# Channel DFT of an FNet plus Mixer layer: products by even and odd channel blocks of 162 columns, their sums on VectorE and GpSimd

## The chip, the cores and the metric

The kernel runs on one core of one Trainium2 chip. The metric is the device time of one execution in microseconds (us); where several runs are given, the median stands with the lowest and the highest beside it. The core has five engines, each with a queue of its own that it works off in order: TensorE (PE in the profile, with its weight loads as PEld), VectorE (DVE), ScalarE (ACT), GpSimd (POOL) and SyncE (SP, which only issues DMA transfers here). Engines wait for each other by semaphores.

## The reference, cut to what matters

The input x has S = 2048 rows (tokens) and D = 640 channels, F is 1728, and everything is fp32:

```python
xn = layernorm(x)
a = einsum("bsd,ed->bse", xn, dft_hid_re)         # DFT along the channels
b = einsum("bsd,ed->bse", xn, dft_hid_im)
fnet = einsum("ts,bse->bte", dft_seq_re, a) - einsum("ts,bse->bte", dft_seq_im, b)
h = layernorm(xn)
u = gelu(einsum("bsd,sf->bdf", h, w1) + b1)       # the MLP runs along the tokens
out = x + fnet + (einsum("bdf,fs->bds", u, w2) + b2).transpose(0, 2, 1)
```

So the output is x, plus the real part of a two-dimensional DFT of the normalized rows, plus a two-layer MLP that mixes tokens.

## The kernel before

**Precision.** An fp32 product is made of three products of a 1-pass type (fp32r). Each matrix is cut into a high part, which ScalarE rounds (`high`, L130), and a low part, the difference, which VectorE makes (`low`, L133). `three` (L138 to L140) then issues high by high, high by low, low by high into one PSUM bank. Every row "PE L138", "L139" or "L140" is one such matmul, and "PEld" of the same line is its weight load.

**Stages.** TensorE runs through them in order: the up projection (w1, with the LayerNorm ahead of it) to about 203.5 us of the profile; the sequence DFT, to 222.7; the channel DFT, to 245.4; the down projection (w2) with the sum of all three terms, to 437.7; then the last rows are stored. The kernel takes the matrices of the reference as inputs and uses the symmetries of DFT matrices: only parts of them are used in the products, and all through the run other parts are loaded and compared with what symmetry says of them (tiles `check`, lines 895 to 983). If one of these comparisons failed, a general version would run at the end.

**The program's order.** Work is a list of `steps`. Step i issues, in this order: its entries of `loads` (DMA), of `reads`, the ScalarE cut for step i + 2, the entries of `middle`, the VectorE cut for step i + 2, the entries of `measures` and `behind`, and last the matmuls of step i. Since every engine works in order, this list fixes what stands behind what in each queue. Entries are put there by `at(step, function, when=list)`.

**The channel DFT** (`hid_step`, `hid_products`). The sequence DFT leaves folded sums in five blocks T0 to T4 (tiles `t_cut`), the moving operand is the channel matrix. Rows and channels have mirror symmetries, so a quarter of the rows suffices: four blocks of 128 rows, named by (odd, i), in the order (1, 0), (1, 1), (0, 0), (0, 1). Each block takes two steps, s = 0 and s = 1, and each step fills two banks (part 0, cosine, and part 1, sine). A bank has 324 columns, 162 for even and 162 for odd channels, and 9 products: `three` by T2 (mixed), by T0 or T3, and by T1 or T4. To make whole rows of 324 columns, each of the four matrices q in `hid_main` is held twice, the second time with alternating sign; the second copy is made by ScalarE on L646 while the sequence DFT runs. In the third block one more bank of 9 products, two rows high, makes the first and the middle row of the output (`mid_bank`, `y_mid`).

**Behind a block.** `copies` (ScalarE, L705) brings both banks of s = 1 to SBUF (tile `sums`), `sums` (VectorE, L709 to L712) makes sum and difference of s = 0 and s = 1, `whole_rows` (VectorE, L663 to L666) turns each into a row block of 640 channels (tile `y`). `read` stores it by SyncE for s = 0 and scatters it by an indirect DMA of GpSimd for s = 1 (L670); `read_back` has ScalarE write it backwards (L727), which is the mirrored row block, and scatters (s = 0) or stores it (s = 1). `read_mid` (ScalarE, L740) does the same for the two special rows. All of it stands two to four steps behind the block's first step, so for the later blocks in the down projection's first steps.

**The down projection.** Sixteen output blocks t of four steps each; a block has 82 products of 320 columns, numbered below by f = 0 to 13, the 128-row slices of w2 (six products for each f, four for f = 13, the short last slice whose low half is stacked beneath). A step needs its cut piece of w2 (`piece`, L130 and L133, from `w_raw`) and the cut of the gelu output, `h_cut0` to `h_cut6`, two slices f each: `h_high` (ScalarE) and `h_low` (VectorE). `h_cut4`, `h_cut5` and `h_cut6` are cut at the end of the channel DFT and in the first two steps of the down projection; GpSimd zeroes 64 rows of `h_cut6` for f = 13 behind its VectorE cut (`h_tail`, L775). Each output block reads its `y` rows back from DRAM (`rest`), adds x, adds the projection (L828, L833) and is stored.

The lines that fix these places:

```python
at(step + 2, copies, when=reads)
at(step + 2, sums, when=reads)
at(step + 2, read(0), when=reads)
at(step + 3, read(1), when=reads)
at(step + 3, read_back(0))
at(step + 4, read_back(1))
order = [(odd, i) for odd in (1, 0) for i in range(NJ)]
at(s_down + 2, h_tail)
```

Of the kernel before, what the change touches and what calls it, by code (L numbers as in the profile page):

```python
# [16 lines left out]
P = 128  # L17
# [32 lines left out]
def fnet_plus_mixer(  # L50
# [579 lines left out]
    def hid_high(q):  # L630
        if not hid_cut:
            hid_cut.append(keep.tile([P, 2, 4, 2, EW], R32, name="hid_main", tag="zt"))
# [3 lines left out]
        nc.scalar.activation(hid_main[:, 0, q, 0], raw[:, q], AF.Copy, scale=by)  # L636
        nc.scalar.activation(hid_mix[:, 0, q], raw[:, 4], AF.Identity, scale=mask[:, q : q + 1])

    def hid_low(q):
        hid_main, hid_mix = hid_cut  # L640
        raw, by = hid_place[0], -1.0 if q > 1 else 1.0
        for to, hi, of, times in (
            (hid_main[:, 1, q, 0], hid_main[:, 0, q, 0], q, by), (hid_mix[:, 1, q], hid_mix[:, 0, q], 4, mask[:, q : q + 1])
        ):
            nc.vector.scalar_tensor_tensor(to, raw[:, of], times, hi.bitcast(F32), op0=ALU.mult, op1=ALU.subtract)
        nc.scalar.activation(hid_main[:, :, q, 1], hid_main[:, :, q, 0].bitcast(F32), AF.Copy, scale=-1.0 if q % 2 else 1.0)  # L646
# [4 lines left out]
    def y_place(n):  # L651

        if n not in y_tiles:
            if n % 6 < 2:
                t = keep.tile([P, 2, 2 * D + 1], F32, name=f"y{n}", tag="n3")
                y_tiles[n - n % 2], y_tiles[n - n % 2 + 1] = t[:, 0], t[:, 1]
# [4 lines left out]
    def whole_rows(y, a, b, e=EW):  # L661
        v = nc.vector
        v.tensor_add(y[:, : e4 + 1], a[:, : e4 + 1], b[:, : e4 + 1])  # L663
        v.tensor_sub(y[:, e4 + 1 : 2 * e4], a[:, e + e4 - 1 : e : -1], b[:, e + e4 - 1 : e : -1])
        v.tensor_add(y[:, 2 * e4 : 3 * e4 + 1], a[:, e : e + e4 + 1], b[:, e : e + e4 + 1])
        v.tensor_sub(y[:, D : 3 * e4 : -1], a[:, :e4], b[:, :e4])  # L666
# [7 lines left out]
    def hid_products(to, w, part, all_blocks=True):  # L674
# [10 lines left out]
    def hid_step(n, odd, i):  # L685
# [16 lines left out]
        def copies():  # L702
            held.append(keep.tile([P, 4, 2 * EW], F32, name=f"sums{n}", tag=f"n{1 + n % 2}"))
# [9 lines left out]

        def read(s):
            def run():
                t, (y, back) = held[0], y_place(2 * n + s)
# [36 lines left out]
        if n == N_MID:  # L753
            at(step + 2, read_mid, when=reads)
# [595 lines left out]
```

## Time and profile before

| what | us |
|---|---|
| median of 3 runs (lowest, highest) | 445.84 (445.72, 446.01) |
| the profiled execution | 445.79 |
| its span, first to last instruction | 443.9 |
| TensorE's granted clock in it, mean | 0.998 |
| sequence DFT, 203.5 to 222.7: TensorE busy of 19.2 | 18.75 |
| channel DFT, 222.7 to 245.4: busy of 22.7: TensorE, VectorE, ScalarE, GpSimd | 22.70, 17.27, 12.44, 4.51 |
| down projection, 245.4 to 437.7: busy of 192.3: the same four | 192.30, 142.74, 96.01, 31.73 |

All times of the profile are of one execution, counted from its first instruction; 1.89 us of the execution lie outside the span. A row by time gives start, length, engine, line, operation, tile written and tiles read; an idle time in brackets at its end is that of the engine just before it, with the engine that ended it. In a row of a group, the number behind x counts instructions, then come busy time and mean ns of one, then idle time. Matmul lengths are modelled and overlap: the distance from one start to the next tells what a matmul takes. The clock row of the page (40 slices) shows 9 throughout, so durations of all stages can be set beside each other.

### The profile page before, as it was taken

The numbers are of one execution on the slowest core, as the hardware profiler recorded it, in microseconds if no ns is written. First come the engines' busy times: TensorE is split into PE (matmuls) and PEld (weight loads), VectorE is DVE, ScalarE is ACT, GpSimd is POOL, SyncE is SP. The second block draws the span as 40 slices with busy tenths as digits, with TensorE's granted clock in tenths as the row PEclk, the third lists the DMA queues.
The fourth block names the chain that finished last, engine by engine and source line by source line (L and its number), as shares of the span: only waits on it lengthen the run. The fifth ranks groups of instructions, "written<-read, shape, count | busy, mean of one in ns | idle before, by whom it ended". The sixth has DMA issues, their size and how long they took to land.

```text
span 443.9 us, 8043 instructions
## 1 busy us (share of the span) xinstructions
PE 434.4 (98%) x2955; PEld 426.8 (96%) x2955; DVE 321.0 (72%) x662; ACT 244.5 (55%) x467; POOL 78.8 (18%) x113
## 2 busy tenths in 40 slices
PE   8999999999999999999999999999999999999994
PEld 4899999999999999999999999999999999999993
DVE  5986634659677787778877947777777769688771
ACT  5566664565656655469645634646455454556440
POOL 2055525710000001100002420102202304101000
PEclk9999999999999999999999999999999999999999
DMA  8692506998665571312107999999998999979401
GB/s 294 222 358 77 189 2 182 312 403 318 199 224 193 190 227 49 117 51 87 46 31 272 291 382 402 397 398 370 329 377 308 313 374 325 376 268 354 149 31 38
DMA packets 49728, 105.71 MB, mean 238 GB/s; under 512 B 7285, under 2 KB 8197, under 8 KB 49681
## 3 DMA queue, kind: packets, MB, share of 16 engines
q1 hardware_dynamic: 46112, 93.53, 60.1%
q0 software_dynamic: 3424, 11.43, 7.1%
q8 instruction: 25, 0.41, 0.4%
q14 instruction: 23, 0.18, 0.1%
q10 hardware_dynamic: 144, 0.16, 0.1%
HBM read 94.60 MB, written 10.51 MB: 237 GB/s over the span
## 4 chain that ended last, share of the span: by engine, by line
PE 79%; DVE 6%; ACT 5%; DMA 3%; issue 3%; POOL 2%; SPq 0%; ACTq 0%; POOLq 0%; DVEq 0%
PE psum L138 25%; PE psum L139 25%; PE psum L140 25%; PE psum L813 2%; DMA w_raw<-in_w 2%; ACT zt L225 2%; DMA xp<-in_x 2%; DVE st L197 1%; POOL r L210 1%; DVE x L133 1%; DVE t L133 1%; ACT q L205 1%; ACT piece L130 1%; PE psum L273 1%; DVE early L133 1%
## 5 line engine op out<-in xcount | busy, mean ns | idle before, releaser
L133 DVE TENSOR_TENSOR piece<-w_raw,piece 128x512 fp32r<-128x512 f32 (+2 forms) x128 | 76.5, 598 | 79.6 <-ACT piece L130 78.2
L138 PE MATMUL psum<-h_cut,piece 128*128 128x320 f32 x416 | 128.6, 309 | 0.0
L140 PE MATMUL psum<-h_cut,piece 128*128 128x320 f32 x416 | 128.4, 309 | 0.0
L139 PE MATMUL psum<-h_cut,piece 128*128 128x320 f32 x416 | 128.3, 308 | 0.0
L130 ACT ACTIVATE piece<-w_raw 128x512 fp32r<-128x512 f32 (+1 forms) x112 | 66.5, 599 | 99.1 <-PE psum L140 57.9
L138 PE MATMUL psum<-x,piece 128*128 128x320 f32 x288 | 88.9, 309 | 0.0
L140 PE MATMUL psum<-x,piece 128*128 128x320 f32 x288 | 88.9, 309 | 0.0
L139 PE MATMUL psum<-x,piece 128*128 128x320 f32 x288 | 88.8, 308 | 0.0
L932 ACT ACTIVATE check<-check 128x1024 f32<-128x1024 f32 (+2 forms) x66 | 65.1, 987 | 34.1 <-DVE check L913 13.4
L138 PEld LDWEIGHTS psum<-h_cut,piece 128*128 128x128 f32 x416 | 78.1, 188 | 0.0
L140 PEld LDWEIGHTS psum<-h_cut,piece 128*128 128x128 f32 x416 | 78.1, 188 | 0.0
L139 PEld LDWEIGHTS psum<-h_cut,piece 128*128 128x128 f32 x416 | 78.1, 188 | 0.0
L273 PE MATMUL psum<-x,early 128*128 128x320 f32 x384 | 58.8, 311 | 2.0 <-DVE early L133 1.1
L273 PEld LDWEIGHTS psum<-x,early 128*128 128x128 f32 x384 | 56.3, 188 | 4.3 <-DVE early L133 1.6
L140 PEld LDWEIGHTS psum<-x,piece 128*128 128x128 f32 x288 | 54.1, 188 | 0.0
L138 PEld LDWEIGHTS psum<-x,piece 128*128 128x128 f32 x288 | 54.1, 188 | 0.0
L139 PEld LDWEIGHTS psum<-x,piece 128*128 128x128 f32 x288 | 54.1, 188 | 0.0
L895 POOL DMA_INDIRECT check<-in_dft_seq,from_seq x16 | 19.7, 1229 | 117.3 <-ACT check L932 114.9
L133 DVE TENSOR_TENSOR x<-zt,x 128x640 fp32r<-128x640 f32 x16 | 13.2, 823 | 12.2 <-ACT x L130 11.5
L670 POOL DMA_INDIRECT y<-y,to_mirror x8 | 9.2, 1146 | 62.0 <-DVE y L666 55.3
L833 DVE SCALAR_TENSOR_TENSOR rest<-psum,b_sb,rest 128x320 f32<-128x320 f32 x32 | 16.1, 544 | 1.0 <-PE psum L813 1.0
L828 DVE TENSOR_TENSOR rest<-rest 128x640 f32<-128x640 f32 x16 | 13.2, 822 | 3.3 <-DMA rest<-in_x 3.1
(197 smaller groups left out, 616.8 us busy)
## 6 DMA issues: line engine op xcount, KB each, us to landing
check<-in_dft_seq SPq DMA_DIRECT2D x58, 512.0 KB
w_raw<-in_w SPq DMA_DIRECT2D x56, 256.0 KB
w_raw<-in_w SPq DMA_DIRECT2D x32, 448.0 KB
rest<-y SPq DMA_DIRECT2D x16, 320.0 KB
rest<-in_x SPq DMA_DIRECT2D x16, 320.0 KB
out<-rest SPq DMA_DIRECT2D x15, 320.0 KB
ck<-in_dft_seq SPq DMA_DIRECT2D x6, 512.0 KB
xp<-in_x SPq DMA_DIRECT2D x8, 320.0 KB
```

Source lines behind the costliest of these rows:

```text
L130: nc.scalar.activation(hi, src, AF.Copy)
L133: nc.vector.tensor_sub(lo, src, hi.bitcast(F32))
L138: nc.tensor.matmul(bank, wh, mh, start=first, stop=False, skip_group_check=True)
L139: nc.tensor.matmul(bank, wh, ml, start=False, stop=False, skip_group_check=True)
L140: nc.tensor.matmul(bank, wl, mh, start=False, stop=last, skip_group_check=True)
L225: nc.scalar.activation(hi if direct else exact[k], rows[k], AF.Identity, scale=by, bias=add)
L273: nc.tensor.matmul(up_banks[f][half][:, :H2], w_cut[f, k // G][part == 2][:, c], n[:, part == 1, k % 2, half * H2 : (half + 1) * H2], star ...
L670: nc.gpsimd.indirect_dma_start(to, bass.IndirectOffsetOnAxis(ap=to_mirror[:, j : j + 1], axis=0), y, None,)
L828: nc.vector.tensor_add(rest[t][:, 0], rest[t][:, 0], rest[t][:, 1])
L833: nc.vector.scalar_tensor_tensor(rest[t][:, 1, cols], down_banks[t][half][:, :H2], b2_sb[:, t : t + 1], rest[t][:, 0, cols], op0=ALU.add, ...
L895: nc.gpsimd.indirect_dma_start(to[:, c * CH : (c + 1) * CH], None, dft_seq.rearrange("c k p t -> (c k p) t"), bass.IndirectOffsetOnAxis(ap ...
L932: nc.scalar.activation(v, v, AF.Square, accum_out=off[:, n : n + 1])
```

## The change

Products are made for each half of a bank apart. `hid_main` holds each matrix once (L646 is gone). T0 (or T3) goes to columns 0 to 161 alone, the even channels, T1 (or T4) to columns 162 to 323, the odd ones: six products of 162 columns. T2 follows with three of 324 columns, with masks that hold the even rows for one half and the odd rows for the other; two more one-column products make these masks at the start.

Now a bank holds an even and an odd part, and sum and difference of the two give the rows. `by_channels` makes them behind `sums`: one addition and one subtraction of 324 columns for part 0 on VectorE and for part 1 on GpSimd (L717, L718). `whole_rows` shrinks from four operations of 159 to 161 columns to two of 320 and 322 (L663, L665). For the two special rows there is one ScalarE copy (L742), two GpSimd sums (L747, L748) and two reversing copies (L751). The tile `sums` has six slots in place of four and other places in SBUF, and `h_cut4` to `h_cut6` too.

The blocks come in another order, (1, 0), (0, 0), (1, 1), (0, 1), so the special rows come with the second block. `read` and `read_back` stand one step later than before for the first two blocks, two for the third and three for the fourth, and each at the end of its step. Two kinds of comparison at the start of the down projection load two and four steps later.

```diff
-        nc.scalar.activation(hid_main[:, :, q, 1], hid_main[:, :, q, 0].bitcast(F32), AF.Copy, scale=-1.0 if q % 2 else 1.0)
...
-    def whole_rows(y, a, b, e=EW):
-        v = nc.vector
-        v.tensor_add(y[:, : e4 + 1], a[:, : e4 + 1], b[:, : e4 + 1])
-        v.tensor_sub(y[:, e4 + 1 : 2 * e4], a[:, e + e4 - 1 : e : -1], b[:, e + e4 - 1 : e : -1])
-        v.tensor_add(y[:, 2 * e4 : 3 * e4 + 1], a[:, e : e + e4 + 1], b[:, e : e + e4 + 1])
-        v.tensor_sub(y[:, D : 3 * e4 : -1], a[:, :e4], b[:, :e4])
+    def whole_rows(y, a, b):
+        back = y[:, D:e4:-1].rearrange("p (h e) -> p h e", h=3)[:, ::2]
+        nc.vector.tensor_sub(back, a[:, :, :e4], b[:, :, :e4])
+        to = y[:, :D].rearrange("p (h e) -> p h e", h=2)
+        nc.vector.tensor_add(to[:, :, : e4 + 1], a[:, :, : e4 + 1], b[:, :, : e4 + 1])
...
-        mix, both = hid_mix[:, :, 2 * part : 2 * part + 2], hid_main[:, :, 2 * part : 2 * part + 2]
-        for block, m in (
-            (T2, mix.rearrange("p h q e -> p h (q e)")), ((T0, T3)[part], both[:, :, 0].rearrange("p h s e -> p h (s e)")),
-            ((T1, T4)[part], both[:, :, 1].rearrange("p h s e -> p h (s e)")),
-        ):
-            three(to, w(block), [m[:, j] for j in range(2)], block == T2, block == (T1, T4)[part])
+        for h, block in enumerate(((T0, T1), (T3, T4))[part]):
+            three(to[:, h * EW : (h + 1) * EW], w(block), [hid_main[:, j, 2 * part + h] for j in range(2)], h == 0, False)
+        m = hid_mix[:, :, 2 * part : 2 * part + 2].rearrange("p h q e -> p h (q e)")
+        three(to, w(T2), [m[:, j] for j in range(2)], False, True)
...
-            held.append(keep.tile([P, 4, 2 * EW], F32, name=f"sums{n}", tag=f"n{1 + n % 2}"))
+            held.append(keep.tile([P, 6, 2 * EW], F32, name=f"sums{n}", tag=("n1", "n2", "n0", "zt")[n]))
...
+        def by_channels():
+            a = held[0].rearrange("p s (h e) -> p (s h) e", h=2)
+            for part, v in enumerate((nc.vector, nc.gpsimd)):
+                even, o = (a[:, 4 * part + h : 4 * part + 4 : 2] for h in range(2))
+                v.tensor_add(a[:, 8 + 2 * part : 10 + 2 * part], even, o)
+                v.tensor_sub(o, even, o)
...
+        def mid_copy():
+            mid = keep.tile([P, D + 2 * EW], F32, name="y_mid", tag="ck1")[0:2]
+            nc.scalar.activation(mid[:, D:], mid_bank[0], AF.Copy)
...
+            nc.gpsimd.tensor_add(y[:, : e4 + 1], even, o)
+            nc.gpsimd.tensor_sub(y[:, 2 * e4 : 3 * e4 + 1], even, o)
...
-        at(step + 2, read(0), when=reads)
-        at(step + 3, read(1), when=reads)
-        at(step + 3, read_back(0))
-        at(step + 4, read_back(1))
+        last = step + (0, 3, 3, 4, 5)[n + 1]
+        at(last - 1, by_channels)
+        for s in range(2):
+            at(last + s, read(s), when=behind)
+            at(last + s + 1, read_back(s))
         if n == N_MID:
-            at(step + 2, read_mid, when=reads)
-
-    order = [(odd, i) for odd in (1, 0) for i in range(NJ)]
+            at(step + 2, mid_copy, when=reads)
+            at(step + 3, read_mid)
+
+    order = [(odd, i) for i in range(NJ) for odd in (1, 0)]
...
-        n = keep.tile([P, 2, 2, D], R32, name=f"h_cut{i}", tag=f"n{(4, 5, 6, 7, 0, 1, 2)[i]}")
+        n = keep.tile([P, 2, 2, D], R32, name=f"h_cut{i}", tag=f"n{(4, 5, 6, 7, 1, 2, 3)[i]}")
...
-            nc.vector.tensor_mul(mask[:, i + 1 : i + 2], mask[:, i : i + 1], parity[:, 2:3])
+            nc.vector.tensor_mul(mask[:, i + 1 : i + 2], mask[:, i : i + 1], parity[:, 1:2])
+            nc.vector.tensor_mul(mask[:, i : i + 1], mask[:, i : i + 1], parity[:, 0:1])
...
-    at(begin, lambda: held_rows.append(quarter_check()), when=loads)
-    at(begin + 3, lambda: quarter_measure(held_rows[0]), when=behind)
+    at(begin + 4, lambda: held_rows.append(quarter_check()), when=loads)
+    at(begin + 6, lambda: quarter_measure(held_rows[0]), when=behind)
...
-        i = begin + 4 + 8 * n
+        i = begin + 6 + 8 * n
```

Three places in the engines' queues follow, each as line, operation, tile written, tiles read and shape. The tiles `sums0` to `sums3` and the `y` tiles are counted by block, two y tiles to a block.

ScalarE at the end of the channel DFT, before: from the copies of the second block to the first piece of w2 cut in the last step but one.

```order
L705 ACTIVATE sums1_2675<-psum3_101 128x324
L705 ACTIVATE sums1_2675<-psum4_102 128x324
L727 ACTIVATE y0_2626<-y0_2626 128x640
L727 ACTIVATE y2_2682<-y2_2682 128x640
L705 ACTIVATE sums2_2745<-psum0_98 128x324
L705 ACTIVATE sums2_2745<-psum1_99 128x324
L740 ACTIVATE y_mid_2758<-psum5_103 2x161
L740 ACTIVATE y_mid_2758<-psum5_103 2x159
L740 ACTIVATE y_mid_2758<-psum5_103 2x161
L740 ACTIVATE y_mid_2758<-psum5_103 2x159
L130 ACTIVATE piece_2765<-w_raw_134 128x512
```

The same place now:

```order
L703 ACTIVATE sums1_2677<-psum4_102 128x324
L703 ACTIVATE sums1_2677<-psum5_103 128x324
L742 ACTIVATE y_mid_2684<-psum1_99 2x324
L733 ACTIVATE y0_2655<-y0_2655 128x640 x2
L751 ACTIVATE y_mid_2684<-y_mid_2684 2x159 x2
L703 ACTIVATE sums2_2745<-psum0_98 128x324
L703 ACTIVATE sums2_2745<-psum1_99 128x324
L130 ACTIVATE piece_2752<-w_raw_134 128x512
```

The third block's copies (`sums2`) stand behind both reversed row blocks of the first block and behind the two `y_mid` copies, which read what GpSimd writes.

GpSimd from the third block's scatters to its MEMSET for `h_cut6`, before:

```order
L670 DMA y1_92<-y5_2788,to_mirror_81 514x640
L670 DMA y3_94<-y4_2752,to_mirror_81 514x640
L670 DMA y1_92<-y6_2830,to_mirror_81 514x640
L670 DMA y3_94<-y6_2830,to_mirror_81 514x640
L775 MEMSET h_cut6_2882 64x640
```

And now, from the first block's second scatter to the MEMSET:

```order
L669 DMA y1_92<-y0_2655,to_mirror_81 514x640
L747 TENSOR_TENSOR y_mid_2684<-y_mid_2684 2x161
L748 TENSOR_TENSOR y_mid_2684<-y_mid_2684 2x161
L669 DMA y3_94<-y2_2721,to_mirror_81 514x640
L669 DMA y1_92<-y3_2757,to_mirror_81 514x640
L717 TENSOR_TENSOR sums2_2745<-sums2_2745 128x324
L718 TENSOR_TENSOR sums2_2745<-sums2_2745 128x2x162
L669 DMA y3_94<-y4_2824,to_mirror_81 514x640
L669 DMA y1_92<-y5_2863,to_mirror_81 514x640
L717 TENSOR_TENSOR sums3_2812<-sums3_2812 128x324
L718 TENSOR_TENSOR sums3_2812<-sums3_2812 128x2x162
L788 MEMSET h_cut6_2859 64x640
```

The MEMSET stood behind the last scatter of all; now the fourth block's two sums stand ahead of it, and that block's two scatters behind it.

VectorE from the cut for the down projection's third step to the low half of `h_cut6`, before:

```order
L133 TENSOR_TENSOR piece_2836<-w_raw_134,piece_2836 128x512
L133 TENSOR_TENSOR h_cut5_2840<-h5_1932,h_cut5_2840 128x1280
L663 TENSOR_TENSOR y6_2830<-sums3_2823 128x161
L664 TENSOR_TENSOR y6_2830<-sums3_2823 128x159
L665 TENSOR_TENSOR y6_2830<-sums3_2823 128x161
L666 TENSOR_TENSOR y6_2830<-sums3_2823 128x160
L133 TENSOR_TENSOR piece_2878<-w_raw_134,piece_2878 128x256
L133 TENSOR_TENSOR piece_2878<-w_raw_134,piece_2878 64x128
L133 TENSOR_TENSOR h_cut6_2882<-h6_2353,h_cut6_2882 128x1280
```

And now, with the two sums behind it:

```order
L133 TENSOR_TENSOR piece_2819<-w_raw_134,piece_2819 128x512
L663 TENSOR_TENSOR y4_2824<-sums2_2745 128x2x160
L665 TENSOR_TENSOR y4_2824<-sums2_2745 128x2x161
L133 TENSOR_TENSOR h_cut5_2821<-h5_1934,h_cut5_2821 128x1280
L133 TENSOR_TENSOR piece_2855<-w_raw_134,piece_2855 128x256
L133 TENSOR_TENSOR piece_2855<-w_raw_134,piece_2855 64x128
L663 TENSOR_TENSOR y5_2863<-sums2_2745 128x2x160
L665 TENSOR_TENSOR y5_2863<-sums2_2745 128x2x161
L133 TENSOR_TENSOR h_cut6_2859<-h6_2351,h_cut6_2859 128x1280
L717 TENSOR_TENSOR sums3_2812<-sums3_2812 128x324
L718 TENSOR_TENSOR sums3_2812<-sums3_2812 128x2x162
```

Between these two cuts stand the rows of the third block in place of those of the fourth, four operations in place of four, but each twice as wide.

More of the change, by code (lines that the diff above doesn't have):

```diff
@@ L631, in hid_high @@
         if not hid_cut:
-            hid_cut.append(keep.tile([P, 2, 4, 2, EW], R32, name="hid_main", tag="zt"))
+            hid_cut.append(keep.tile([P, 2, 4, EW], R32, name="hid_main", tag="zt"))
             hid_cut.append(keep.tile([P, 2, 4, EW], R32, name="hid_mix", tag="ck0"))
@@ L635, in hid_high @@
         raw, by = hid_place[0], -1.0 if q > 1 else 1.0
-        nc.scalar.activation(hid_main[:, 0, q, 0], raw[:, q], AF.Copy, scale=by)
+        nc.scalar.activation(hid_main[:, 0, q], raw[:, q], AF.Copy, scale=by)
         nc.scalar.activation(hid_mix[:, 0, q], raw[:, 4], AF.Identity, scale=mask[:, q : q + 1])
@@ L642, in hid_low @@
         for to, hi, of, times in (
-            (hid_main[:, 1, q, 0], hid_main[:, 0, q, 0], q, by), (hid_mix[:, 1, q], hid_mix[:, 0, q], 4, mask[:, q : q + 1])
+            (hid_main[:, 1, q], hid_main[:, 0, q], q, by), (hid_mix[:, 1, q], hid_mix[:, 0, q], 4, mask[:, q : q + 1])
         ):
             nc.vector.scalar_tensor_tensor(to, raw[:, of], times, hi.bitcast(F32), op0=ALU.mult, op1=ALU.subtract)
-        nc.scalar.activation(hid_main[:, :, q, 1], hid_main[:, :, q, 0].bitcast(F32), AF.Copy, scale=-1.0 if q % 2 else 1.0)
     e4 = D // 4
@@ L653, in y_place @@
         if n not in y_tiles:
-            if n % 6 < 2:
+            if n < 2:
                 t = keep.tile([P, 2, 2 * D + 1], F32, name=f"y{n}", tag="n3")
-                y_tiles[n - n % 2], y_tiles[n - n % 2 + 1] = t[:, 0], t[:, 1]
+                y_tiles[0], y_tiles[1] = t[:, 0], t[:, 1]
             else:
@@ L712, in sums @@
             v.tensor_sub(t[:, 3], t[:, 3], banks[1])
+        def by_channels():
[4 more added lines that the diff above has]
+                v.tensor_sub(o, even, o)
         def read(s):
             def run():
-                t, (y, back) = held[0], y_place(2 * n + s)
-                whole_rows(y, t[:, s], t[:, 2 + s])
+                a, (y, back) = held[0].rearrange("p s (h e) -> p (s h) e", h=2), y_place(2 * n + s)
+                whole_rows(y, a[:, 8 + s : 2 * s : s - 7], a[:, 10 + s : 4 + 2 * s : s - 5])
                 if s:
@@ L732, in read_back @@
             return run
+        def mid_copy():
+            mid = keep.tile([P, D + 2 * EW], F32, name="y_mid", tag="ck1")[0:2]
+            nc.scalar.activation(mid[:, D:], mid_bank[0], AF.Copy)
+            mid_bank.append(mid)
         def read_mid():
-            a, y = mid_bank[0], keep.tile([P, D], F32, name="y_mid", tag="ck1")[0:2]
-            for to, of in (
-                (y[:, : e4 + 1], a[:, : e4 + 1]), (y[:, 2 * e4 - 1 : e4 : -1], a[:, EW + 1 : EW + e4]),
-                (y[:, 2 * e4 : 3 * e4 + 1], a[:, EW : EW + e4 + 1]), (y[:, D - 1 : 3 * e4 : -1], a[:, 1:e4]),
-            ):
-                nc.scalar.activation(to, of, AF.Copy)
+            y, (even, o) = mid_bank[1][:, :D], (mid_bank[1][:, D + h * EW :][:, : e4 + 1] for h in range(2))
+            nc.gpsimd.tensor_add(y[:, : e4 + 1], even, o)
+            nc.gpsimd.tensor_sub(y[:, 2 * e4 : 3 * e4 + 1], even, o)
+            for h in range(2):
+                begin = 2 * e4 * h
+                nc.scalar.activation(y[:, D - 1 - begin : 3 * e4 - begin : -1], y[:, begin + 1 : begin + e4], AF.Copy)
             for s in range(2):
```

2 lines of the change are left out of this document (1 added, 1 removed).

## The prediction

> **What bounds the kernel now.** Read first the page's busy times, then the chain of work that ended last, in order of time, then TensorE's rows by time.
>
> ```profile
> PE 434.4 (98%) x2955; PEld 426.8 (96%) x2955; DVE 321.0 (72%) x662; ACT 244.5 (55%) x467; POOL 78.8 (18%) x113
> ```
> ```profile
> 222.54 0.36 PE psum L592 x3
> 256.94 0.58 PE psum L813 x4
> ```
>
> The chain (start, length, engine, line) runs from 222.54 to 256.94 us without another engine's row: the whole channel DFT and the first output block are TensorE's alone. So what TensorE saves there ends the kernel sooner, as long as nobody else becomes late. TensorE's own rows (start, length, line, operation, in brackets the idle time before) give the spacing:
>
> ```profile
> 206.28 0.39 PE L139 MATMUL psum<-piece,f 128*128 128x256 f32 x1 [0.36 <-DVE piece L133]
> ...
> 213.24 0.28 PE L138 MATMUL psum<-piece,f 128*128 128x256 f32 x1
> ...
> 217.46 0.28 PE L138 MATMUL psum<-piece,f 128*128 128x258 f32 x1
> ...
> 222.74 0.31 PE L138 MATMUL psum<-hid_mix,t 128*128 128x324 f32 x1
> ...
> 245.36 0.31 PE L138 MATMUL psum<-h_cut,piece 128*128 128x320 f32 x1
> ...
> 255.90 0.31 PE L138 MATMUL psum<-h_cut,piece 128*128 128x320 f32 x1
> ```
>
> A row's length overlaps its neighbours; spacing is what counts. The channel DFT holds 17 banks of 9 products, 153 in (245.36 - 222.74) us: 0.1478 us for one of 324 columns. The 36 of 256 columns from 213.24 to 217.46 take 0.1172 us each. The last row is f = 12 of the first output block, 72 products of 320 columns behind 245.36: 0.1464 us each.
>
> **TensorE's part.** Six of a bank's nine products fall from 324 to 162 columns: 96 short ones in 16 banks and 6 in the bank for the middle row. No matmul under 256 columns of this type is in the trace. By columns alone a short one would be spaced 0.1478 x 162/324 = 0.074 us. But each has its own weight load:
>
> ```profile
> L140 PEld LDWEIGHTS psum<-hid_main,t 128*128 128x128 f32 x32 | 6.0, 188 | 0.0
> ...
> L139 PEld LDWEIGHTS psum<-hid_main,t_mid_cut 128*2 128x2 f32 x2 | 0.2, 84 | 0.1
> L592 PEld LDWEIGHTS psum<-own 65*65 65x65 f32 x1 | 0.1, 135 | 0.0
> ```
>
> From 2 to 128 columns a load (mean ns behind the bar) grows by (188 - 84)/126 = 0.83 ns a column, so 128 columns may hold the load path 0.106 us whatever streams past; loads do keep up at 0.117 us, as the 256-column rows show. I take 0.112 us, between these two, and 0.08 us in the middle bank, whose loads are two columns wide. A bank then costs 6 x 0.112 + 3 x 0.148 = 1.115 us in place of 1.33, and TensorE's part is 96 x 0.036 + 6 x 0.068 = 3.9 us shorter. Bounds: 0.074 us (7.5 us saved) and, if loads and products stop overlapping, the 0.188 us of a load (4.1 us lost).
>
> The four negating copies on ScalarE go too. One row each of ScalarE and VectorE by time:
>
> ```profile
> 201.36 0.47 ACT L646 ACTIVATE hid_main<-hid_main 128x324 fp32r<-128x324 f32 x1 [0.69 <-DVE hid_main L645]
> ```
> ```profile
> 204.13 1.49 DVE L133 TENSOR_TENSOR h_cut<-h,h_cut 128x1280 fp32r<-128x1280 f32 x1 [0.48 <-ACT h_cut L130]
> ```
>
> The copy kept ScalarE 0.69 us waiting and some 0.4 us busy; behind it ScalarE cuts the h_cut for which VectorE idles 0.48 us, and behind that comes the piece for which TensorE idles 0.36 us at 206.28. I count that 0.36 us as gone, bound below by nothing: the channel DFT starts at 222.38. Two more one-column mask products lie near 69 us, where TensorE has work queued: nothing.
>
> So TensorE alone would be 4.2 us ahead at 241.15. **What is late next** decides how much of it stays.
>
> **The engines behind.** POOL did no sums before. Its nearest rows (mean ns), and its stretch by time:
>
> ```profile
> L212 POOL TENSOR_SCALAR again<-mv,again 128x1 f32<-128x1 f32 x11 | 2.9, 262 | 1.1
> ...
> L775 POOL MEMSET h_cut<- 64x640 f32 x1 | 0.6, 633 | 0.0
> ...
> L407 POOL MEMSET zt<- 128x4 f32 x2 | 0.1, 102 | 0.0
> ```
> ```profile
> 244.89 0.97 POOL L670 DMA_INDIRECT y<-y,to_mirror  x1 [5.41 <-DVE piece L133]
> 246.16 1.10 POOL L670 DMA_INDIRECT y<-y,to_mirror  x1 [0.30 <-ACT sums L705]
> 252.44 0.97 POOL L670 DMA_INDIRECT y<-y,to_mirror  x1 [5.18 <-DVE y L666]
> 253.72 2.13 POOL L670 DMA_INDIRECT y<-y,to_mirror  x1 [0.30 <-ACT h_cut L130]
> 255.89 0.63 POOL L775 MEMSET h_cut<- 64x640 f32 x1
> ```
>
> A MEMSET grows by (633 - 102)/636 = 0.83 ns a column, 0.27 us for 324; on top of the 0.26 us of an arithmetic instruction a sum takes 0.53 us with one such pass, 1.07 with three (two reads, one write). I take two passes, 0.8 us. The Trainium skill's GPSIMD Engine Reference (3.1 Elementwise) states about 2.6 cycles at 1.2 GHz an element for a two-input add; an estimate from that is 0.70 us for 324 and a gain 0.3 us larger than below; no run here shows it yet. A scatter holds POOL 1.3 us (252.44 to 253.72).
>
> VectorE's rows by time for the stretch that matters:
>
> ```profile
> 242.61 0.69 DVE L133 TENSOR_TENSOR piece<-w_raw,piece 128x512 fp32r<-128x512 f32 x1
> 243.21 0.33 DVE L663 TENSOR_TENSOR y<-sums 128x161 f32<-128x161 f32 x1
> ...
> 246.34 0.48 DVE L709 TENSOR_TENSOR sums<-psum,sums 128x324 f32<-128x324 f32 x1
> ...
> 248.19 0.32 DVE L663 TENSOR_TENSOR y<-sums 128x161 f32<-128x161 f32 x1
> ...
> 253.51 1.49 DVE L133 TENSOR_TENSOR h_cut<-h,h_cut 128x1280 fp32r<-128x1280 f32 x1 [0.69 <-ACT h_cut L130]
> 254.92 0.69 DVE L133 TENSOR_TENSOR piece<-w_raw,piece 128x512 fp32r<-128x512 f32 x1
> ```
>
> From start to next start: a piece 0.60 us, the four sums of two banks 1.85, an h_cut 1.41. The new 320 to 324 column operations lie between 0.38 (by columns of the piece) and 0.46 (a quarter of the four sums): 0.41. Note the slack before: h_cut6 is ready at 254.9, TensorE wants it at 255.90. One microsecond. If TensorE comes four earlier, VectorE is late.
>
> Now the queues as the change orders them. The third block's ScalarE copies stand behind both reversed rows of the first block and two y_mid copies that wait for POOL. TensorE ends the second block (with the middle bank) at 222.38 + 8 x 1.115 + 0.92 = 232.2. ScalarE copies it and the middle bank, and reverses the first row by 233.8. POOL: scatter to 235.15, two sums to 236.75, scatter to 238.05, two short y_mid sums (0.8 together) to 238.85. ScalarE's y_mid copies (0.2 each) and its first copy of the third block end at 239.7. So VectorE starts the third block's sums at 239.75, though TensorE had the block ready at 236.7. They end at 241.6, the first piece at 242.2: TensorE starts the down stage at 242.3, not at 241.15.
>
> Then VectorE's queue without rest: two row sums 0.82, two channel sums 0.82, piece 0.60, about 0.5 idle until ScalarE has cut h_cut4, h_cut4 1.41, four sums 1.88, piece 0.61, rows 0.82, h_cut5 1.41, split piece 0.63, rows 0.82: from 242.25 to 252.6; h_cut6 to 254.0. TensorE can start f = 12 at 254.05 and f = 13 six products later, if the rows of POOL's MEMSET are there. POOL: scatter behind the rows of 252.6, to 253.9; the fourth block's two sums, to 255.5; MEMSET 0.63, to 256.2. TensorE starts f = 13 at 256.25. Before it did so at 255.90 + 6 x 0.1464 = 256.78. **Of 4.2 us there remain 0.5.** Behind that the stage is TensorE's again, with the same products as before.
>
> The same count with other values: POOL's sum at 0.53 us gains 1.6, at 1.07 it loses 0.6. Short products at 0.074 us gain 2.0, and 3.2 with POOL at 0.53; at 0.117 nothing. Transfers: the same bytes; the second block of w2 moves behind one y store, to about 238, and is wanted at 247; the first check loads move two to four steps later. Nothing.
>
> The sum is made on the profiled execution, 445.79 us with a span of 443.9; the median is 445.84. 445.79 - 0.5 = **445.3 us**.
>
> **Rivals.**
> 1. *VectorE and POOL hold each other up*, 446.7 us. Speaks for it: the scatter beside the h_cut of 253.51 lasted 2.13 us, not 0.97. Against: others beside VectorE's work, 244.89 among them, were not longer. Place: the third block's two POOL sums fall beside the piece and h_cut4. If VectorE stands for them, 1.6 us less its 0.5 idle, h_cut6 ends at 255.0; the fourth block's two sums take turns with h_cut6 and one channel sum: 255.0 + 0.8 + 0.41 + 0.8 + 0.63 = 257.6, f = 13 is 0.9 later than before. Decides from the point where the held time passes 0.5 us. With sums of 0.53 it gains 0.8 (445.0), with 1.07 it loses 2.9 (448.7). The Trainium skill's SBUF — State Buffer (Who interferes with whom) states just this: a VectorE instruction with two SBUF inputs and a GpSimd instruction that reads SBUF exclude each other for a whole instruction. By that page the time would be the 446.7 of this rival; no run here has shown such a pair.
> 2. *Short products are not shorter*, 447.3 to 461.5 us. Nothing of this width is in the trace, so a spacing of its own can't be excluded. At 0.148 us TensorE saves nothing and the queue behind it still costs 1.5. At 0.311, the whole length of a 324-column row, 96 x 0.163 = 15.7 us are lost. Decides from 0.148 us. Against it: spacing follows columns from 320 to 256.
> 3. *The queue behind is shorter than counted*, 442.6 to 444 us: POOL near 0.5 us, short products near 0.074, no turns taken. Then 1.8 to 3.2 us stay.
>
> **Chances.** The forecast (444.6 to 446.4, POOL's bounds) 0.45, rival 1 0.28, rival 2 0.15, rival 3 0.12. The range takes in all but rival 2's greater part and the outer ends: 442.6 to 448.7. A difference of 0.2%, 0.9 us, is about what a measurement tells from none. Faster by more: two fifths of the forecast, all of rival 3, a little of rival 1: 0.32. Slower by more: half of rival 1, rival 2, a little of the forecast: 0.30. Within: 0.38.
>
> **What would show it.** Right: spacing of the 162-column rows near 0.11 us; the channel stage about 19 us long; idle time of TensorE before the first piece, before h_cut5 or h_cut6 and before f = 13 of the first output block, released by VectorE and POOL; none later. Wrong: short rows at 0.15 us or more; POOL sums far from 0.8 us; VectorE's rows longer than before beside POOL's sums (rival 1); no idle time at all (rival 3); idle time in later output blocks, for which I see no cause.

## The result: slower by 0.94%, and the profile after

The changed kernel takes 450.16 us (median of 6 runs, 448.33 to 451.33), the kernel before 445.86 us (6 runs, 445.72 to 446.12): ratio 1.0094, 95% interval 1.0072 to 1.0116. That is above the whole range of the prediction, and on the other side of no change than its forecast. The profiled execution took 451.33 us with a span of 449.5 us and a mean clock of 0.989.

First the page's busy times, then the view by stretches. Its columns are the stretch, its length, the busy time and count of TensorE, its weight loads, VectorE, ScalarE and GpSimd, then the granted clock, the DMA share and GB/s.

```profile
PE 435.1 (97%) x2955; PEld 426.3 (95%) x2955; DVE 328.9 (73%) x656; ACT 243.8 (54%) x462; POOL 88.6 (20%) x123
222.30:241.20 18.90, 18.90 (x155) 18.45 (x153) 15.24 (x35) 8.62 (x24) 6.43 (x8) 1.00 0.18 71
241.20:259.50 18.30, 12.88 (x80) 11.60 (x79) 17.96 (x27) 9.18 (x14) 9.29 (x9) 0.98 0.84 282
259.50:265.90 6.40, 6.38 (x24) 6.38 (x25) 4.47 (x9) 1.37 (x2) 2.30 (x2) 0.51 1.02 393
```

The channel DFT fills TensorE and is shorter (18.9 us; 22.7 before). In the first output block the roles are turned: VectorE is busy 17.96 of 18.30 us, TensorE 12.88. And in the next 6.4 us, with TensorE busy again, its clock is 0.51.

TensorE's rows by time (start, length, line, operation, idle time before; "..." stands for rows left out):

```profile
222.41 0.28 PE L139 MATMUL psum<-hid_main,t 128*128 128x162 f32 x1
222.52 0.28 PE L140 MATMUL psum<-hid_main,t 128*128 128x162 f32 x1
...
241.37 0.38 PE L138 MATMUL psum<-h_cut,piece 128*128 128x320 f32 x1 [0.16 <-DVE sums L708]
242.80 0.41 PE L140 MATMUL psum<-h_cut,piece 128*128 128x320 f32 x1 [0.91 <-DVE piece L133]
...
250.76 0.42 PE L140 MATMUL psum<-h_cut,piece 128*128 128x320 f32 x1 [0.66 <-DVE piece L133]
...
253.10 0.41 PE L139 MATMUL psum<-h_cut,piece 128*128 128x320 f32 x1 [0.46 <-DVE h_cut L133]
...
256.21 0.41 PE L139 MATMUL psum<-h_cut,piece 128*128 128x320 f32 x1 [1.10 <-DVE h_cut L133]
...
257.05 0.31 PE L826 MATMUL psum<-h_cut,piece 128*128 128x320 f32 x1
259.52 1.17 PE L826 MATMUL psum<-h_cut,piece 128*128 128x320 f32 x3 [2.17 <-POOL h_cut L788]
260.49 0.47 PE L138 MATMUL psum<-h_cut,piece 128*128 128x320 f32 x1
260.75 0.47 PE L139 MATMUL psum<-h_cut,piece 128*128 128x320 f32 x1
...
265.93 0.31 PE L138 MATMUL psum<-h_cut,piece 128*128 128x320 f32 x1
```

Short products start 0.11 us apart. The down projection starts at 241.37, 3.99 us earlier than before (245.36). Then come five more stalls in its first block, each released by VectorE or, the longest, by GpSimd's MEMSET of `h_cut6` (L788). The first product of f = 13 needs only the high half and runs at 257.05; the second needs the zeroed rows and runs at 259.52, where all four had started at 256.78 before. From 260.49 on products start 0.27 us apart in place of 0.15; at 265.93 the usual length is back.

VectorE's and GpSimd's rows of that stretch:

```profile
234.69 1.64 DVE L663 TENSOR_TENSOR y<-sums 128x320 f32<-128x320 f32 x1
...
244.53 1.74 DVE L133 TENSOR_TENSOR piece<-w_raw,piece 128x512 fp32r<-128x512 f32 x1
246.20 2.04 DVE L133 TENSOR_TENSOR h_cut<-h,h_cut 128x1280 fp32r<-128x1280 f32 x1
...
254.26 0.50 DVE L665 TENSOR_TENSOR y<-sums 128x322 f32<-128x322 f32 x1
254.67 1.49 DVE L133 TENSOR_TENSOR h_cut<-h,h_cut 128x1280 fp32r<-128x1280 f32 x1
256.07 0.49 DVE L717 TENSOR_TENSOR sums<-sums 128x324 f32<-128x324 f32 x1
256.60 1.56 DVE L718 TENSOR_TENSOR sums<-sums 128x324 f32<-128x324 f32 x1
258.08 1.24 DVE L133 TENSOR_TENSOR piece<-w_raw,piece 128x512 fp32r<-128x512 f32 x1
```
```profile
237.58 0.99 POOL L669 DMA_INDIRECT y<-y,to_mirror  x1 [0.64 <-DVE y L665]
...
244.96 0.77 POOL L717 TENSOR_TENSOR sums<-sums 128x324 f32<-128x324 f32 x1
245.80 1.10 POOL L718 TENSOR_TENSOR sums<-sums 128x324 f32<-128x324 f32 x1
...
255.03 1.97 POOL L669 DMA_INDIRECT y<-y,to_mirror  x1 [1.14 <-DVE y L665]
257.03 0.76 POOL L717 TENSOR_TENSOR sums<-sums 128x324 f32<-128x324 f32 x1
257.87 0.90 POOL L718 TENSOR_TENSOR sums<-sums 128x324 f32<-128x324 f32 x1
258.83 0.63 POOL L788 MEMSET h_cut<- 64x640 f32 x1
```

Beside GpSimd's sums of 244.96 and 245.80 (the third block's) a piece lasts 1.74 us in place of 0.69 and the cut of `h_cut4` 2.04 in place of 1.49. VectorE's own sum beside the one of 257.03 lasts 1.56 us, its neighbour 0.49, and the piece of 258.08 lasts 1.24 (0.69 is usual). The row operation of 234.69 stands beside the second block's sums on GpSimd (235.20 and 236.05) and lasts 1.64 us, where 0.49 is usual; the scatter of 237.58 waits 0.64 us for these rows. At the end the MEMSET follows a scatter of 1.97 us and two sums.

### The profile page after: what moved, and what is told of

It reads as the page before. It is cut to its first block, busy times and chain, and to the rows that moved or that the text cites. A ratio compares the mean times of both kernels' runs of the same rounds, so it can differ in the third digit from the quotient of the medians.

```text
span 449.5 us, 8052 instructions
## 1 busy us (share of the span) xinstructions
PE 435.1 (97%) x2955; PEld 426.3 (95%) x2955; DVE 328.9 (73%) x656; ACT 243.8 (54%) x462; POOL 88.6 (20%) x123
## 4 chain that ended last, share of the span: by engine, by line
PE 82%; DVE 6%; DMA 4%; issue 2%; ACT 2%; POOL 1%; POOLq 0%; ACTq 0%; DVEq 0%
PE psum L138 23%; PE psum L139 23%; PE psum L140 23%; PE psum L273 9%; DMA y<-y,to_mirror 3%; PE psum L826 2%; PE psum L263 2%; DVE st L197 1%; DMA xp<-in_x 1%; DVE early L133 1%; DVE x L133 1%; ACT t L130 1%; DVE t L133 1%; DMA w_raw<-in_w 1%; POOL y L669 0%
## 5 line engine op out<-in xcount | busy, mean ns | idle before, releaser
L133 DVE TENSOR_TENSOR piece<-w_raw,piece 128x512 fp32r<-128x512 f32 (+2 forms) x128 | 78.1, 610 | 81.9 <-ACT piece L130 80.6
L139 PEld LDWEIGHTS psum<-h_cut,piece 128*128 128x128 f32 x416 | 79.2, 190 | 2.1 <-DVE h_cut L133 2.1
L140 PEld LDWEIGHTS psum<-h_cut,piece 128*128 128x128 f32 x416 | 79.1, 190 | 2.1 <-DVE piece L133 2.1
L138 PEld LDWEIGHTS psum<-h_cut,piece 128*128 128x128 f32 x416 | 79.2, 190 | 0.4 <-ACT piece L130 0.4
L909 POOL DMA_INDIRECT check<-in_dft_seq,from_seq x16 | 21.2, 1326 | 104.7 <-ACT check L946 102.2
L927 DVE TENSOR_TENSOR check<-check,check 128x512 f32<-128x512 f32 x24 | 15.5, 686 | 0.0
```

Of the source, the lines that this page charges most:

```text
L133: nc.vector.tensor_sub(lo, src, hi.bitcast(F32))
L138: nc.tensor.matmul(bank, wh, mh, start=first, stop=False, skip_group_check=True)
L139: nc.tensor.matmul(bank, wh, ml, start=False, stop=False, skip_group_check=True)
L140: nc.tensor.matmul(bank, wl, mh, start=False, stop=last, skip_group_check=True)
L909: nc.gpsimd.indirect_dma_start(to[:, c * CH : (c + 1) * CH], None, dft_seq.rearrange("c k p t -> (c k p) t"), bass.IndirectOffsetOnAxis(ap ...
L927: (v.tensor_add if odd != (i == 4 and m) else v.tensor_sub)(x1, x0, x1)
```

## The experiments

Two theories were set against each other. **Turns**: a sum on GpSimd stops VectorE for as long as it works, so VectorE, which is the bound there, loses more than the sum would cost it. **Queue**: GpSimd's rows only stand in the wrong order, and VectorE has too much to do in any case. A third question was where the time lost from 260 to 266 us and the spread of 3 us between runs come from. Times are medians with the lowest and highest; ratios are against the kernel before on the same chips, with their 95% intervals.

### All channel sums on VectorE

```diff
-            for part, v in enumerate((nc.vector, nc.gpsimd)):
+            for part, v in enumerate((nc.vector, nc.vector)):
```

> VectorE makes the channel sums of part 1 too, GpSimd none. Theory 'turns' (a sum on GpSimd holds VectorE up for as long as it lasts, some 0.85 us, so VectorE loses more by it than the 0.47 us that the sum would cost on VectorE itself): VectorE's rows L663 and pieces L133 keep their usual length everywhere, the fourth block's MEMSET comes about 3 us earlier, f = 13 starts near 257, and without a drop of the clock the time is 445.9 to 447. Rival 'queue' (VectorE was simply late, and what it does not hand to GpSimd makes it later): four more sums a block on VectorE, 8 x 0.47 = 3.8 us up to f = 13, so 450 or more. If the clock falls after the remaining idle time, up to 3 us on top in either theory.

Measured: 445.33 us (445.05 to 445.75, 10 runs), ratio 0.9987 (0.9978 to 0.9997). TensorE's, VectorE's and GpSimd's rows by time:

```profile
255.91 0.71 PE L826 MATMUL psum<-h_cut,piece 128*128 128x320 f32 x3 [0.37 <-POOL h_cut L788]
```
```profile
244.33 0.69 DVE L133 TENSOR_TENSOR piece<-w_raw,piece 128x512 fp32r<-128x512 f32 x1
244.93 1.49 DVE L133 TENSOR_TENSOR h_cut<-h,h_cut 128x1280 fp32r<-128x1280 f32 x1
```
```profile
253.21 1.97 POOL L669 DMA_INDIRECT y<-y,to_mirror  x1 [1.15 <-DVE y L665]
255.22 0.63 POOL L788 MEMSET h_cut<- 64x640 f32 x1
```

VectorE does two more sums a block (eight in all, as the expectation counts, though it says four a block) and is done earlier: the same piece and the same cut have their usual length, the second product of f = 13 starts at 255.91, 3.6 us earlier (0.5 us of that lies ahead of the stage: its first short product starts at 221.82 in this execution, 222.33 in the other). The stall of 1.10 us for `h_cut6` is still there (at 254.39); those of 242.80 and 253.10 have their counterparts too, the one of 250.76 is gone. The time is 0.6 us better than the lower end of Turns; Queue had 450 or more, and falls. The edit also takes two sums from ahead of the MEMSET, which the next experiment separates. The scatter of 253.21 still lasts 1.97 us, with no sum on GpSimd; so its length is not from the sums. It lies beside the cut of `h_cut6` here too, which the ninth experiment takes up.

### The MEMSET ahead of the fourth block's sums

```diff
-    at(s_down + 2, h_tail)
+    middle[s_down + 2].insert(0, h_tail)
```

> The MEMSET of h_cut6 stands ahead of the fourth block's two sums on GpSimd, everything else as in the changed kernel. If the two sums ahead of it cost what the profile shows (257.03 to 258.83), f = 13 starts 1.8 us earlier, near 257.7, TensorE idles 0.4 us there instead of 2.17, and the clock need not fall: 446.5 to 448. If the MEMSET waits for something else that shares the queue (the scatter of 255.03), nothing changes: 450.

Measured: 446.54 us (446.42 to 448.73, 10 runs), ratio 1.0023 (1.0012 to 1.0033); nine of the ten lie within 0.6 us. TensorE's row, then GpSimd's:

```profile
257.64 0.71 PE L826 MATMUL psum<-h_cut,piece 128*128 128x320 f32 x3 [0.38 <-POOL h_cut L788]
```
```profile
256.95 0.63 POOL L788 MEMSET h_cut<- 64x640 f32 x1
257.67 1.29 POOL L717 TENSOR_TENSOR sums<-sums 128x324 f32<-128x324 f32 x1
```

The stall before the second product of f = 13 is 0.38 us, not 2.17: the two sums ahead of the MEMSET were worth 1.8 us of it. Nine of the ten runs have a mean clock of 0.995 or more, the long one 0.992.

### Part 1's channel sums left out

```diff
-            for part, v in enumerate((nc.vector, nc.gpsimd)):
+            for part, v in enumerate((nc.vector,)):
...
-                whole_rows(y, a[:, 8 + s : 2 * s : s - 7], a[:, 10 + s : 4 + 2 * s : s - 5])
+                whole_rows(y, a[:, 8 + s : 2 * s : s - 7], a[:, 4 + 2 * s : 6 + 2 * s])
```

> The channel sums of part 1 are left out, and the rows read the part 1 operands without them; all else is as in the changed kernel. Theory 'turns': this takes away both the held time and the two sums ahead of the MEMSET; the down projection starts near 241, f = 13 near 254.5, the time is 443 to 444.5. Rival 'queue': only the two sums ahead of the MEMSET go, f = 13 near 257.7, 447 to 448.

Measured: 443.77 us (443.61 to 444.04, 4 runs), ratio 0.9954 (0.9938 to 0.9971). The down projection starts at 241.08, the second product of f = 13 at 255.08, 0.6 us later than expected. This kernel leaves these sums out of its rows; it only tells what they cost. GpSimd's sums cost 6.4 us of the 450.16 in all, the clock's part and the waits for their results included, more than the 4 us that TensorE had won. VectorE making them itself costs 1.6 us (first experiment).

### Rows of the late blocks behind the cuts

```diff
-            for part, v in enumerate((nc.vector, nc.gpsimd)):
+            for part, v in enumerate((nc.vector, nc.vector)):
...
-        at(step + 2, copies, when=reads)
-        at(step + 2, sums, when=reads)
-        last = step + (0, 3, 3, 4, 5)[n + 1]
-        at(last - 1, by_channels)
+        at(step + (2, 2, 2, 5)[n], copies, when=reads)
+        at(step + (2, 2, 2, 5)[n], sums, when=reads)
+        at(step + (2, 2, 3, 5)[n], by_channels)
         for s in range(2):
-            at(last + s, read(s), when=behind)
-            at(last + s + 1, read_back(s))
+            last = ((3, 5), (5, 6), (11, 11), (11, 12))[n][s] + s_hid
+            at(last, read(s), when=behind)
+            at(last + 1, read_back(s))
```

> All channel sums on VectorE, the fourth block's copies and sums three steps later, the rows of the third and fourth block behind h_cut6 (and one row block of the first a step later). If the loss is only the order of VectorE's and GpSimd's work at the start of the down projection, TensorE keeps its lead: first product of the down projection near 241.3, no idle time of over 0.3 us up to the second output block, 441.4 to 443, with a clock near 0.998. If the loss lies in the work itself (VectorE has too much of it wherever it stands), idle time comes back one or two output blocks later, and the time is 445 or more.

Measured: 442.69 us (442.25 to 445.90, 10 runs), ratio 0.9939 (0.9922 to 0.9955). The first product of the down projection starts at 240.87, and no stall of 0.1 us follows until 278:

```profile
278.64 0.42 PE L140 MATMUL psum<-h_cut,piece 128*128 128x320 f32 x1 [1.32 <-DVE piece L133]
```
```profile
277.16 0.83 DVE L841 TENSOR_TENSOR rest<-rest 128x640 f32<-128x640 f32 x1 [3.71 <-DMA rest<-in_x]
```

So VectorE has time for all of it, only not there. Of the lead of 4.49 us over the kernel before at the start of the down projection, 2.55 us are left at its last product. VectorE waited 3.71 us for the rows of x and y of the third output block, and the pieces of w2 behind that wait came late.

### The wait filled with matmuls

```diff
+                if t == 0 and last and half == 0:
+                    for _ in range(6 if f < NF else 12):
+                        nc.tensor.matmul(psum[(bank_turn[0] + 2) % 8][:, :H2], idle[:, :P], idle[:, :H2], start=True, stop=True)
```

> The changed kernel with 18 more matmuls of 320 columns of ones, whose sums nobody reads, in TensorE's queue where it waits: 6 ahead of f = 12 and 12 ahead of f = 13 of the first output block. They lie within the idle time (1.10 and 2.17 us), so f = 13 starts where it did or up to 0.3 us later. Theory 'clock': the run to run spread of the changed kernel (448.3 to 451.3) is the granted clock, which falls to 0.50 because TensorE idles there; kept busy, it stays at 1.00, and all runs lie near 448.3 to 448.8. Rival: the fall has nothing to do with the idle time (it comes with the rest of the load at that place); then the spread stays and the median is 450 or more.

Measured: 448.43 us (448.01 to 448.49, 4 runs), ratio 1.0056 (1.0039 to 1.0073). TensorE's row where the second product of f = 13 starts, and the stretch behind it:

```profile
259.45 0.70 PE L829 MATMUL psum<-h_cut,piece 128*128 128x320 f32 x3 [0.48 <-POOL h_cut L788]
```
```profile
259.50:265.90 6.40, 6.40 (x44) 6.40 (x45) 5.63 (x12) 2.42 (x4) 2.30 (x2) 1.00 1.03 400
```

The products start where they did (259.45, 259.52 in the changed kernel), the clock stays at 1.00, and the spread is gone. Without the clock's fall the changed kernel is 2.65 us slower than the kernel before (448.43 against 445.78 on that chip): its stalls cost TensorE's whole lead and this on top. The clock's fall is the rest, 1.7 us in the median run and 2.9 us in the profiled one. The rival, that the clock falls with the other load at that place, is out: the transfers and the other engines' rows are the same here (DMA share 1.03, 1.02 in the changed kernel), and only TensorE's idle time is filled.

### Late rows, but GpSimd sums

The fourth experiment's kernel with the first line of its diff left as it was.

> As e4 (later rows, later fourth block), but part 1's channel sums on GpSimd again. Here no sum stands ahead of the MEMSET of h_cut6. Theory 'turns': what is left of GpSimd's harm is the time for which its sums hold VectorE: the third block's sums come late again, the first product of the down projection starts 2.5 to 3 us later than in e4 (near 243.5), idle time comes again in the second output block beside the fourth block's sums, and the time is 444.5 to 446.5. Rival 'queue' (GpSimd harmed only by what stood ahead of the MEMSET): as e4, 442 to 443.

Measured: 444.57 us (444.27 to 449.05, 7 runs), ratio 1.0001 (0.9967 to 1.0034). The time is as Turns had it, one of the two places is not:

```profile
261.11 0.42 PE L140 MATMUL psum<-h_cut,piece 128*128 128x320 f32 x1 [0.41 <-DVE piece L133]
...
279.54 0.42 PE L140 MATMUL psum<-h_cut,piece 128*128 128x320 f32 x1 [1.19 <-DVE piece L133]
```
```profile
243.12 1.74 DVE L133 TENSOR_TENSOR piece<-w_raw,piece 128x512 fp32r<-128x512 f32 x1
```

The down projection starts at 240.81, as without GpSimd's sums, so the late start was expected wrongly. The piece of 243.12 is held as long as in the changed kernel, but nobody waits for it. The harm comes at 261.11, in the second output block, as expected. Beside the fourth block's sums (253.65 and 254.58 on GpSimd) a sum of VectorE lasts 0.94 us and the next operation 1.38, where 0.50 and 0.82 are usual; from there VectorE works without a pause to the piece of 260.38, for which TensorE waits. The stall of 279.54 answers to the one of 278.64 above, and one of 0.23 us follows at 292.05. The median is 1.9 us above the fourth experiment's (444.57 against 442.69); two of the seven runs, at 447.99 and 449.05 us, had a mean clock of 0.990.

### The sum of x and y a step later

```diff
-        at(len(steps) + 2 + (t == 0), rest_sum, t)
+        at(len(steps) + 3, rest_sum, t)
```

on top of the fourth experiment's edits.

> As e4, and the sum of y and x in each output block one step later for all blocks but the first, where it is there already. In e4 VectorE stood at that sum for 3.71 us at 277.16 until the rows had landed, the next piece of w2 behind it came late, and TensorE idled 1.32 us (and its next products came 0.3 to 0.6 us late). If that is where e4 lost the rest of its lead, the time is 440.8 to 441.6. If the transfers bind there whatever VectorE does, 442.3 to 442.8, with idle time elsewhere.

Measured: **441.18 us** (441.05 to 441.31, 4 runs), ratio 0.9895 (0.9878 to 0.9911). No stall of 0.1 us from 240 to 294 us. The down projection starts at 240.90, and its last product lies 4.4 us ahead of the one before. This kernel is faster than the kernel before and the changed one.

### A probe of the turns

The last kernel, with work on GpSimd that nobody reads in the quiet later blocks:

```diff
...
+        for _ in range(12):
+            if kind == 0:
+                g.tensor_sub(t[:, 4], t[:, 0], t[:, 1])
+            elif kind == 1:
+                g.memset(t[:, 4:6], 0.0)
+            else:
+                g.tensor_copy(t[:, 4], t[:, 0])
...
+    for kind in range(3):
+        at(s_down + 30 + 8 * kind, probe, kind)
```

> As e7, with work on GpSimd that nobody reads, in later output blocks, at 12 instructions a time: at the ninth block's start sums of two tiles in SBUF (324 columns), two blocks later MEMSETs of 648 columns, two blocks after that copies of 324 columns. Theory 'turns': beside the sums VectorE's rows with two SBUF operands (pieces, usually 0.69 us in the records) last 1.3 to 2 us, and both engines together get done one engine's work at a time; beside the copies, which read SBUF too, the same in part; ScalarE's rows keep their length. Rival (no turns, the rows of the changed kernel were long for another reason, say the transfers): pieces stay at 0.69 us in all three places.

Measured: 440.80 us (one run). VectorE's rows for the same line (comparisons of two tiles in SBUF), beside sums, beside MEMSETs, beside copies and beside nothing, then a line that reads PSUM, beside sums and beside nothing, with the piece that follows it amid the sums; last GpSimd's own:

```profile
328.20 2.68 DVE L946 TENSOR_TENSOR check<-check 128x512 f32<-128x512 f32 x2
353.60 1.29 DVE L946 TENSOR_TENSOR check<-check 128x512 f32<-128x512 f32 x2
369.14 1.80 DVE L946 TENSOR_TENSOR check<-check,check 128x512 f32<-128x512 f32 x2
387.44 1.28 DVE L946 TENSOR_TENSOR check<-check 128x512 f32<-128x512 f32 x2
...
326.68 1.00 DVE L846 SCALAR_TENSOR_TENSOR rest<-psum,b_sb,rest 128x320 f32<-128x320 f32 x2
327.60 0.68 DVE L133 TENSOR_TENSOR piece<-w_raw,piece 128x512 fp32r<-128x512 f32 x1
385.92 1.00 DVE L846 SCALAR_TENSOR_TENSOR rest<-psum,b_sb,rest 128x320 f32<-128x320 f32 x2
```
```profile
318.09 16.00 POOL L879 TENSOR_TENSOR probe<-probe 128x324 f32<-128x324 f32 x12
348.48 8.34 POOL L881 MEMSET probe<- 128x648 f32 x12
367.18 9.30 POOL L883 COPY probe<-probe 128x324 f32<-128x324 f32 x12
```

Two operations with operands in SBUF take 1.28 us alone, 1.29 beside MEMSETs, 1.80 beside copies and 2.68 beside sums. Operations that take one operand from PSUM keep their 1.00 us. Twelve sums take GpSimd 16.00 us, 1.33 each, where two in a row had started 0.84 us apart in the changed kernel (257.03 and 257.87). Both sides pay. TensorE, with pieces cut ahead, has no stall of 0.1 us here.

### The cut ahead of the rows

On top of the first experiment's edit, the low cut of `h_cut6` is issued ahead of the third block's second rows, which stood before it in the same list:

```diff
-        at(when, h_low, i, when=behind)
+        behind[when].insert(0 if i == 6 else len(behind[when]), lambda i=i: h_low(i))
```

> As the first experiment (all channel sums on VectorE), and the low cut of h_cut6 stands ahead of the third block's second rows on VectorE, so that GpSimd's scatter of those rows no longer begins inside that cut of 1.49 us but beside channel sums of 0.49 us each. If a VectorE operation that is under way holds the scatter up until it ends, the scatter lasts 1.0 to 1.3 us in place of 1.97. If its length has another cause (the scatter ahead of it, the transfers), it stays near 1.97. The MEMSET stands behind it in either case, and the rows before it come 1.4 us later, so the time is no better than the first experiment's: 445.5 to 446.5.

Measured: 445.44 us (one run). GpSimd's row of the scatter in question:

```profile
254.79 0.97 POOL L669 DMA_INDIRECT y<-y,to_mirror  x1 [2.55 <-DVE y L665]
```

It lasts 0.97 us, not 1.97: what holds a scatter is the long VectorE operation inside which it begins. The time is as in the first experiment, as expected, since the scatter now waits for the later rows instead: the stall for `h_cut6` shrinks from 1.10 to 0.17 us, and the one before the second product of f = 13 grows from 0.37 to 1.70.

## Why the prediction was wrong, step by step

**TensorE's part** was right. A bank was put at 1.115 us with short products 0.112 us apart; they start 0.11 us apart. The channel DFT was to start at 222.38 and started at 222.33; its last product starts at 240.90, so the 17 banks end within 0.1 us of the forecast for TensorE alone (241.15). The idle time of 0.36 us at 206.28 went as counted.

**The idea that VectorE and GpSimd are late next, and where**, was right: the stalls lie at the first piece, at `h_cut5` and `h_cut6` and at f = 13, released by the engines that were named, and none comes later. One more, of 0.66 us at a later piece (250.76), was not named.

**The step that failed is the sum over "VectorE's queue without rest" and GpSimd's queue**, which put f = 13 at 256.25 by adding each engine's durations as if the other were not there. It came at 259.52, 3.27 us later. Row by row:

- VectorE was to end the third block's rows at 252.6 and ended them near 254.67: 2.1 us. The piece and the cut beside GpSimd's sums took 1.05 and 0.55 us more, less the idle time of 0.5 us that had been counted there: 1.1. Another 0.4 us is a later start, which has the same cause one block earlier: the rows of 234.69 were held beside the second block's sums, the scatter of 237.58 waited 0.64 us for them, and the `y_mid` sums behind it on GpSimd and the third block's copies behind those on ScalarE came later. The rest is 0.1 us on each of four pairs of row or channel operations (0.93 us, not 0.82) and 0.15 us on the split piece.
- The scatter behind them was to hold GpSimd 1.3 us and took from 254.67 to 257.03, 2.4: another 1.1. It waited for the rows to 255.03, and it begins inside the cut of `h_cut6`, which holds it up (1.97 us; 0.97 in the ninth experiment).
- GpSimd's two sums took 1.8 us from 257.03 to 258.83, not 1.6 (and not the 1.4 that 0.70 us a sum would give): 0.2.

The second of these stood in the prediction's own rows. It quoted a scatter of 2.13 us before, and set the one of 244.89 (0.97) against it. VectorE's row by time in the kernel before shows what parts them:

```profile
244.91 1.50 DVE L133 TENSOR_TENSOR h_cut<-h,h_cut 128x1280 fp32r<-128x1280 f32 x1
```

The short scatter began 0.02 us ahead of VectorE's operation, the long one 0.21 us behind the start of its own (253.72, 253.51). The scatter of 246.16 (1.10 us), also quoted there, began inside the cut of 244.91, 0.25 us before that ended. Both it and the long one end some 0.85 us behind the operation inside which they begin (247.26 against 246.41, 255.85 against 255.00), and so does the one of 255.03 in the changed kernel (257.00 against 256.16). So the row of 244.89 was no counter-evidence.

So this was **rival 1, with too low a price**. It had the mechanism, the place and f = 13 late by 0.9 us against before. Measured were 2.74 us (259.52 against 256.78), and 2.65 us in the time without the clock's fall (fifth experiment). That GpSimd's sums hold VectorE is shown by the first experiment and the probe, what the two sums ahead of the MEMSET cost by the second, that VectorE holds the scatter by the ninth. Rival 1 gave VectorE's queue the time for which it is held beside the third block's sums, and left out the time for which the scatter is: of the 1.8 us that it fell short (the MEMSET done at 259.46, not 257.6), 1.1 lay in a `h_cut6` that came at 256.07, not 255.0, by the sizes above, and the rest in the scatter. The Trainium skill's SBUF — State Buffer (Who interferes with whom), which rival 1 named beside its sum, has a VectorE instruction with two SBUF inputs and a GpSimd instruction that reads SBUF shut each other out, but not one that only writes. The probe agrees for sums (2.68 against 1.28 us) and for MEMSETs (1.29), and in part for copies, which read SBUF too (1.80). Operations with one operand from PSUM went on beside the sums (1.00 us). Not every operation pays: the piece of 327.60, amid the sums, kept its 0.68 us, and why stays open.

**What no case held is the clock.** The prediction took every duration at the full clock, since that was 0.998 before. In the kernel before, TensorE had not idled in this stretch. In the profiled execution a stall of 2.17 us, after shorter ones, was followed by 0.51 of the clock for 6.4 us, and some 20 products took nearly twice their time: from f = 13 of the first output block to f = 13 of the second it took 14.9 us (259.52 to 274.42 in the chain of waits), not 12.0. These 2.9 us are what parts 451.33 us from the 448.43 of the fifth experiment; in the median run it is 1.7 us. Without the clock's fall the time would have been inside the range, near its upper end.

The range failed since the worst case of rival 1 was built with a dearer sum (448.7 us) and not with what else would wait, and since nothing in it stood for what a stall does to TensorE afterwards. One slip in the sums changed nothing: with GpSimd's sum at 0.53 us the count gains 1.6 us, which is 444.2 us and not the 444.6 with which the forecast's band begins.

## What to carry to other kernels

Work given to GpSimd need be no relief for a VectorE that is the bound. Here VectorE makes a sum of 324 columns in 0.47 us (four in a row from 242.45 to 244.33 in the first experiment). Beside the two sums that GpSimd made of the second, third and fourth block, VectorE's operations took 1.6 us more for each pair (1.15 + 0.43, 1.05 + 0.55 and 1.07 + 0.55): 0.8 us a sum. When TensorE becomes faster, look for what its waits were covering, and move what nobody needs soon behind what is waited for: the same arithmetic took 450.16 us in one order and 441.18 us in another, with less of it on GpSimd. And a stall of TensorE can cost more than its length: the one of 2.17 us was followed by up to 2.9 us more at half the clock, in some runs by none.

## What was not expected of the hardware

The granted clock fell to half of full speed within an idle time of 2.17 us, with 1.10, 0.46 and 0.66 us of idle time in the 9 us ahead of it: it is 1.00 from 257.30 to 258.50, 0.70 in the next us and 0.50 from 259.50 to 262.00. It was back at full by 265.93. The changed kernel's six runs had mean clocks of 0.989 to 0.999, the lowest for the two longest and the highest for the shortest. The Trainium skill's TensorE: Matmul & The Clock Gate (Why this matters for your kernels) asks for no idle gaps above some 3 us; by that this gap should have been harmless, and the measurement decides. Single runs of kernels whose profiles show a longest stall of 1.1 to 1.3 us were long at a lower mean clock too: one of ten in the second experiment (448.73 us at 0.992), one of ten in the fourth (445.90 at 0.992), two of seven in the sixth (447.99 and 449.05 at 0.990). Against that, none of the ten runs of the first experiment and the four of the third, with a stall of 1.10 us in their profiles, was, and the one run of the ninth kept its clock at 1.00 through a stall of 1.70 us (254.60 to 263.00). What length of stall suffices stays open.
